# Attention with a threshold, then a feed-forward layer, on one core: scores from split q and k instead of float32 row halves

## The chip, the core and the metric

The kernel runs on one core of a Trainium2 chip. The core has five engines that each work through their own instructions in order: TensorE (PE, with its weight loads listed as PEld), VectorE (DVE), ScalarE (ACT), GpSimd (POOL) and SyncE (SP), which here issues all transfers. The metric is the device time of one execution in microseconds; the time before is the median of 3 runs, 1317.29 us (1316.47 to 1318.95).

## The reference

```
# q, k, v: (8, 8, 576, 64); w_in: (512, 2048); w_out: (2048, 512)
scores = scale * q @ k^T                       # scale = 64 ** -0.5
scores = where(scores >= max(scores) - tau, scores, -1e9)
attn   = exp(scores - max); attn /= sum(attn) + 1e-9
x      = (attn @ v), heads side by side        # 4608 x 512
out    = (s * relu(x @ w_in) ** 2 + b) @ w_out
```

## The kernel before

A **visit** is one batch entry, one pair of heads (2 of 8) and one half `u` of the first 512 query rows: 8 x 4 x 2 = 64 visits, four to a pair (batch, u). Each visit has four **tiles** of 128 query rows by 576 keys; half the visits have a fifth tile for the last 64 query rows of both heads (the tail). There are 288 tiles.

A tile goes through: scores on PE into a PSUM bank `s0` or `s1` (L205-222), scaling with the minimum on DVE into `sm` (L230), exp on ACT into `em` (L240), the threshold with the sum on DVE (L243), a reciprocal, the normalisation on POOL (L247), 32x32 block transposes on DVE into `tr` (L266, L268), and four transfers from `tr` to `er` which put the blocks in place (L272). The first four visits transpose on PE instead (L250-263). After a visit's last tile `with_v` multiplies v by `er` into `pv` (L284), and ACT copies the result to the x buffer `xb` (L288).

The scores are float32. k of both heads lies on the 128 partitions, 64 for each head, as does q; two products on the upper and lower rows of the array give a tile of each head (L220). The tail multiplies a block-diagonal `qd` by k (L211). `with_v` writes the two heads to the two column halves of the array.

The feed-forward layer (FFN) works on **blocks** of 256 rows: 16 full ones, one for each (batch, u), and two made of the tails (`xt`). A block is staged, that is, x is split into `xh` (rounded to float32r) and `xl` (the rest) by ACT and DVE (L398, L400). Then come 16 steps: 12 products of 256 columns into `h` (L415), relu, square and rounding on ACT (L418-421), the rest `gl` on POOL (L422), and 6 products of 512 columns into `o` (L428). There are three x buffers, and two pairs of `xh`/`xl`.

Nothing of the order is left to chance: all work is handed to `Plan` with an engine, a cost, keys that it reads and writes, and a due time `at` in tiles. `Plan.run` goes through it with these costs, gives each free engine the ready work with the smallest `at`, and so fixes each engine's order. SP's queue is ordered in the same way (L169).

Of the kernel before, what the change touches and what calls it, by code (L numbers as in the profile page):

```python
# [101 lines left out]
def tile_attention_ffn(ctx: ExitStack, tc: tile.TileContext, qT, kT, v, tau, w_in, w_out, s, b, out):  # L102
# [68 lines left out]

    class Visit:
        def __init__(self, n, bi, pair, u, tail):
            self.n, self.bi, self.pair, self.u, self.tail, self.end = n % 2, bi, pair, u, tail, False
# [4 lines left out]
            self.nb = (NB + (T if tail else 0)) // 32
            self.pe = n < PE_VISITS  # L180

        def load(self, at):
# [1 line left out]
            dma(295, lambda: nc.sync.dma_start(out=kb[n], in_=kT[bi, h2].rearrange("h d s -> (h d) s")), [], [("k", n)], at)
            dma(131, lambda: nc.sync.dma_start(out=qb[n], in_=qT[bi, h2, :, self.u * NB:(self.u + 1) * NB].rearrange(
                "h d s -> (h d) s")), [], [("q", n)], at)
            if self.tail:
                for j in range(2):
                    dma(16, lambda j=j: nc.sync.dma_start(out=qd[n][j * D:(j + 1) * D, j * T:(j + 1) * T],
                                                          in_=qT[bi, 2 * self.pair + j, :, M:S]), [], [self.kd[j]], at)  # L190
            for j in range(2):
                rows = "(p c) d -> p c d" if self.pe else "(c p) d -> p c d"
                dma(131, lambda j=j, rows=rows: nc.sync.dma_start(
                    out=vb[n][:, j, 0:NQ], in_=v[bi, 2 * self.pair + j, 0:M, :].rearrange(rows, p=P)),
                    [], [self.kv[j]], at + 1)
# [4 lines left out]
            for m in range(2):  # L200
                dma(16, lambda m=m: nc.sync.dma_start(  # L201
                    out=vb[n][:, :, NQ].rearrange("(k m) h d -> k m h d", m=4)[:, m],
                    in_=v[bi, h2, M + 32 * m:M + 32 * m + 32, :].rearrange("h k d -> k h d")), [], [self.kv[2 + m]], at + 1)
# [19 lines left out]

    def tile_of(vs, i, j, t):
        ps, ks_, st8 = bank[f"s{j}"], f"st{i % 6}", st[i % 6]
# [50 lines left out]
    def with_v(vs, at):  # L276
        n, nb = vs.n, vs.nb
        ps = bank["pv"]

        def products():  # L280
            for c in range(5):
                r = slice(0, T if vs.pe and c == NQ else P)
                for j in range(2):
                    nc.tensor.matmul(ps[j * D:(j + 1) * D, 0:32 * nb], vb[n][r, j, c], er[r, n, j, 0:nb, 32 * c:32 * c + 32],  # L284
                                     start=(c == 0), stop=(c == 4))
        pe(10.5 * 0.85 * 32 * nb, products, vs.kv + [("er", n, j, e) for j in range(2) for e in range(nb)], ["pv"], at)
        xk = xs[vs.bi, vs.u]
        act((340, 420), lambda: nc.scalar.copy(out=xb[xk][:, vs.pair], in_=ps[:, 0:NB]), ["pv"],  # L288
            [("x", xk, vs.pair)] + (["ident"] if xk == 2 else []), at)
# [26 lines left out]
    def weights(f, at):  # L316
# [6 lines left out]
        tag = ("xh", "xl")[f % 2] + ("01"[f // 2 % 2] if f < FIRST_WEIGHTS else "1")  # L323
# [19 lines left out]
        for u, k in (0, "i"), (1, "o"):  # L343
            kr, kt = (f"w{f}", k), (tag, u)
            act((665, 750), lambda u=u: nc.scalar.activation(
                out=tmp()[:, u], in_=words(1, u).bitcast(F32), func=AF.Prelu, scale=2.0 ** -112, alpha=-2.0 ** 32),
                [kr], [kt] if u else [tag, kt, (tag, 1)], at)
            dve2((480, 550), lambda u=u: nc.vector.tensor_scalar(
                out=y(u), in0=y(u), scalar1=3, scalar2=None, op0=ALU.logical_shift_left), [kt], [kt], at)
            dve2((700, 780), lambda u=u: nc.vector.scalar_tensor_tensor(  # L350
                out=y(u), in0=words(0, u), scalar=29, in1=y(u), op0=ALU.logical_shift_right, op1=ALU.bitwise_or),
                [kr, kt], [kt], at)
        for u, k in (0, "i"), (1, "o"):
            act((615, 700), lambda u=u: nc.scalar.copy(out=w()[:, u, 0], in_=tmp()[:, u]), [(tag, u)],
# [24 lines left out]

    class Block:  # L380
# [3 lines left out]
        def stage(self, at):  # L384

            k = count["stage"] % 2
            count["stage"] += 1
            self.kx = [f"xh{k}", f"xl{k}"]

            def get():  # L390
                if self not in lazy:
                    lazy[self] = [sb(t, [P, NC, NB], F32R) for t in self.kx]
                return lazy[self]
            self.get = get
            for c in range(0, NC, 2):
                sl = slice(c, c + 2)
                kh, kl = (self.kx[0], c // 2), (self.kx[1], c // 2)
                act((520, 620), lambda sl=sl: nc.scalar.copy(out=get()[0][:, sl], in_=self.src[:, sl]),  # L398
                    self.ksrc, [kh] if c else self.kx + [(x, u) for x in self.kx for u in range(2)], at)
                dve2((620, 700), lambda sl=sl: nc.vector.tensor_tensor(  # L400
                    out=get()[1][:, sl], in0=self.src[:, sl], in1=get()[0][:, sl].bitcast(F32), op=ALU.subtract),
                    self.ksrc + [kh], [kl], at)

        def step(self, f, at):
# [3 lines left out]
            kx = self.kx + [(x, c) for x in self.kx for c in range(2)]  # L408

            def products():  # L410
                xh, xl = self.get()
                i = 0
                for c in range(NC):
                    for w, x in ((wi[0][f], xh), (wi[0][f], xl), (wi[1][f], xh)):
                        nc.tensor.matmul(ps, w[:, c, :], x[:, c, :], start=(i == 0), stop=(i == 3 * NC - 1))  # L415
                        i += 1
            pe(3 * NC * 120.5, products, kx + [(f"w{f}", "i")], ["h"], at)
            act((290, 385), lambda: nc.scalar.activation(out=g, in_=ps, func=AF.Relu), ["h"], [f"g{k}"], at)  # L418
# [3 lines left out]
            do((715, 750), lambda: eng.tensor_tensor(out=lo, in0=g, in1=hi.bitcast(F32), op=ALU.subtract),  # L422
# [7 lines left out]
            for t in range(2):  # L430
                pe(3 * 232, lambda t=t: second(t), [f"gh{k}", f"gl{k}", (f"w{f}", "o")],
                   [("o", t)] + (["o"] if f == 0 and t == 0 else []), at + 1)

        def finish(self, at):
            for t in range(2):
                k, o = "oo", oo

                def take(t=t, o=o):
                    nc.vector.scalar_tensor_tensor(out=o, in0=bank["o"][:, t, :], scalar=s_t, in1=bias_t, op0=ALU.mult,  # L439
                                                   op1=ALU.add)  # L440
# [82 lines left out]
    for i, (vs, j, t) in enumerate(tiles):  # L523
        if t is None or not j:
# [76 lines left out]
```

## Time and profile before

| | |
|---|---|
| median of 3 runs | 1317.29 us |
| profiled execution | 1318.1 us, span 1316.1 us |
| mean granted clock of PE | 0.986 |
| DMA packets, bytes | 271470, 164.17 MB |
| issues of er, v, k, q, qd | 1088, 128 + 120 + 4, 64, 64, 64 |

The slices of the span show three parts:

```profile
PE   7689799999999999999999999999999999999997
DVE  6888876666676766657575656766666576663011
ACT  5666545545455555555455554555555455554343
PEclk8999899999999999999999999999999999999999
```

Each column is a fortieth of the span, 33 us, each digit a busy share in tenths. In the first five or six DVE is busiest, as the weights are converted beside the first visits. Then PE is. In the last three or four the attention is over (DVE falls to nothing), and the last FFN blocks run. A busy digit of PE doesn't say that it works at its peak: starts of products show that better. SP is not in these sums: what its queue does is read from its issues in order of time.

### The profile page before, as it was taken

How to read it: one execution, taken by the hardware profiler on the slowest of the kernel's cores; microseconds unless marked ns; L12 is line 12 of the kernel's file. 1: busy time of each engine (PE TensorE's matmuls, PEld its weight loads, DVE VectorE, ACT ScalarE, POOL GpSimd, SP SyncE). 2: the span in 40 equal slices, each digit the busy share in tenths (PEclk: the TensorE clock that was granted, in tenths of full speed). 3: DMA queues.
4: the chain of work that ended last, by engine and by line, in shares of the span. 5: the costliest groups of instructions: out<-in, count | busy, mean ns of one | idle time of the engine just before them, and what ended most of it. 6: DMA issues, size and time to landing. Idle time of an engine off the chain costs nothing.

```text
span 1316.1 us, 24095 instructions
## 1 busy us (share of the span) xinstructions
PE 1254.2 (95%) x7752; PEld 972.6 (74%) x7752; DVE 824.5 (63%) x2157; ACT 684.6 (52%) x1655; POOL 551.0 (42%) x613
## 2 busy tenths in 40 slices
PE   7689799999999999999999999999999999999997
PEld 5366567677677777777777777777787778787886
DVE  6888876666676766657575656766666576663011
ACT  5666545545455555555455554555555455554343
POOL 3676534344444444434344343534445344443210
PEclk8999899999999999999999999999999999999999
DMA  7844455545555455544454444544445444542000
GB/s 226 297 155 118 119 138 130 136 122 125 142 135 142 124 137 127 142 113 122 124 135 122 124 123 112 152 114 125 127 129 133 116 118 126 137 113 60 17 17 17
DMA packets 271470, 164.17 MB, mean 125 GB/s; under 512 B 99824, under 2 KB 256496, under 8 KB 271344
## 3 DMA queue, kind: packets, MB, share of 16 engines
q1 hardware_dynamic: 271344, 162.63, 46.5%
q8 instruction: 62, 1.02, 0.3%
q14 instruction: 64, 0.52, 0.1%
HBM read 63.96 MB, written 9.44 MB: 56 GB/s over the span
## 4 chain that ended last, share of the span: by engine, by line
PE 77%; DVE 7%; DMA 4%; SPq 4%; issue 3%; ACT 3%; POOL 1%; DVEq 0%; POOLq 0%; ACTq 0%
PE o L428 27%; PE h L415 27%; PE pv L284 12%; PE s L220 9%; SPq L272 3%; DMA er<-tr 3%; PE s L211 2%; DVE em L243 1%; DVE sm L230 1%; ACT em L240 1%; DMA out_dram<-oo 1%; DVE tr L266 1%; DVE xl L350 1%; DVE oo L439 1%; SPq L201 1%
## 5 line engine op out<-in xcount | busy, mean ns | idle before, releaser
L415 PE MATMUL h<-xh,w 128*128 128x256 f32 x2304 | 478.3, 290 | 18.7 <-ACT g L418 12.2
L247 POOL TENSOR_SCALAR em<-em,st,zero 128x576 f32<-128x576 f32 x288 | 283.2, 984 | 391.0 <-DVE st L246 236.7
L415 PEld LDWEIGHTS h<-xh,w 128*128 128x128 f32 x2304 | 379.4, 192 | 65.0 <-ACT g L420 20.4
L428 PE MATMUL o<-w,gh 128*128 128x512 f32 x1152 | 370.9, 403 | 3.4 <-DVE oo L439 3.4
L422 POOL TENSOR_TENSOR gl<-g,gh 128x256 fp32r<-128x256 f32 x272 | 222.7, 820 | 304.8 <-issue 136.1
L415 PE MATMUL h<-xl,w 128*128 128x256 f32 x1152 | 327.1, 284 | 0.3 <-DVE xl L400 0.3
L240 ACT ACTIVATE em<-sm,st 128x576 f32<-128x576 f32 x288 | 222.7, 774 | 192.7 <-DVE sm L230 125.7
L243 DVE SCALAR_TENSOR_TENSOR em<-sm,st,em 128x577 f32<-128x577 f32 x288 | 250.3, 870 | 89.0 <-ACT st L238 54.1
L230 DVE TENSOR_SCALAR_CACHE_REDUCE sm<-s,nsc 128x576 f32<-128x576 f32 x288 | 227.2, 808 | 121.6 <-PE s L220 83.4
L266 DVE STREAM_TRANSPOSE tr<-em 128x512 f32<-128x512 f32 x272 | 192.7, 709 | 144.9 <-DMA er<-tr 78.7
L428 PEld LDWEIGHTS o<-w,gh 128*128 128x128 f32 x1152 | 199.6, 189 | 68.1 <-issue 22.1
L418 ACT ACTIVATE g<-h 128x256 f32<-128x256 f32 x288 | 109.4, 380 | 266.2 <-PE h L415 258.9
L428 PE MATMUL o<-w,gl 128*128 128x512 f32 x576 | 225.5, 391 | 2.6 <-POOL gl L422 2.6
L415 PEld LDWEIGHTS h<-xl,w 128*128 128x128 f32 x1152 | 220.9, 192 | 8.4 <-DVE xl L400 0.6
L284 PE MATMUL pv<-er,v 128*64 128x256 f32 (+1 forms) x1280 | 185.2, 416 | 8.6 <-DMA er<-tr 5.4
L220 PE MATMUL s<-k,q 64*128 64x288 f32 x1024 | 167.0, 437 | 6.5 <-DVE sm L230 6.5
L284 PEld LDWEIGHTS pv<-er,v 128*64 128x64 f32 x1280 | 95.0, 138 | 87.1 <-issue 26.3
L428 PEld LDWEIGHTS o<-w,gl 128*128 128x128 f32 x576 | 108.2, 188 | 30.1 <-POOL gl L422 5.2
L220 PEld LDWEIGHTS s<-k,q 64*128 64x128 f32 x1024 | 93.3, 190 | 47.9 <-DVE sm L230 10.9
L421 ACT CAST gh<-g 128x256 fp32r<-128x256 f32 x288 | 115.8, 402 | 13.5 <-PE o L428 7.4
L420 ACT ACTIVATE g<-g 128x256 f32<-128x256 f32 x288 | 119.3, 414 | 6.5
L238 ACT ACTIVATE st<-st,tau 128x1 f32<-128x1 f32 x272 | 76.7, 286 | 26.3 <-DVE sm L230 26.0
(56 smaller groups left out, 532.2 us busy)
## 6 DMA issues: line engine op xcount, KB each, us to landing
er<-tr SPq DMA_DIRECT2D x1088, 80.0 KB, 2.2
k<-in_k_dram SPq DMA_DIRECT2D x64, 288.0 KB, 3.1
v<-in_v_dram SPq DMA_DIRECT2D x128, 128.0 KB, 2.5
q<-in_q_dram SPq DMA_DIRECT2D x64, 128.0 KB, 2.4
w<-in_moe_w_in_dram SPq DMA_DIRECT2D x16, 512.0 KB, 7.0
w<-in_moe_w_out_dram SPq DMA_DIRECT2D x16, 512.0 KB, 7.3
out_dram<-oo SPq DMA_DIRECT2D x32, 256.0 KB, 2.3
v<-in_v_dram SPq DMA_DIRECT2D x120, 16.0 KB, 2.1
```

The lines of the kernel that those rows point to most:

```text
L220: nc.tensor.matmul(bank[f"s{j}"][:, hf, 0:HS], qb[n][r, t * P:(t + 1) * P], kb[n][r, cs], start=True, stop=True)
L230: dve((745, 830), lambda: nc.vector.tensor_scalar(out=sb_[:, 0:S].rearrange("p (a b) -> p a b", a=2), in0=ps[:, :, 0:HS], scalar1=nsc, sca ...
L240: act((780, 870), lambda: nc.scalar.activation(out=ev, in_=sb_[:, 0:S], func=AF.Exp, bias=st8[:, 0:1], scale=-1.0), [sm_k, (ks_, 0)], [em_ ...
L243: dve2((940, 1010), lambda: nc.vector.scalar_tensor_tensor(out=eb, in0=sb_, scalar=st8[:, 1:2], in1=eb, op0=ALU.is_le, op1=ALU.mult, accum ...
L247: pool((900, 940), lambda: nc.gpsimd.tensor_scalar(out=ev, in0=ev, scalar1=st8[:, 4:5], scalar2=zero, op0=ALU.mult, op1=ALU.add), [em_k, ( ...
L266: nc.vector.transpose(out=to[:, :, 0:NQ].rearrange("p m c q -> p m (c q)"), in_=ev[:, 0:M].rearrange("p (m r) -> p m r", m=4))
L284: nc.tensor.matmul(ps[j * D:(j + 1) * D, 0:32 * nb], vb[n][r, j, c], er[r, n, j, 0:nb, 32 * c:32 * c + 32], start=(c == 0), stop=(c == 4))
L415: nc.tensor.matmul(ps, w[:, c, :], x[:, c, :], start=(i == 0), stop=(i == 3 * NC - 1))
L420: act((290, 390), lambda: nc.scalar.activation(out=g, in_=g, func=AF.Square), [f"g{k}"], [f"g{k}"], at)
L421: act((310, 405), lambda: nc.scalar.copy(out=hi, in_=g), [f"g{k}"], [f"gh{k}"], at)
L422: do((715, 750), lambda: eng.tensor_tensor(out=lo, in0=g, in1=hi.bitcast(F32), op=ALU.subtract), [f"g{k}", f"gh{k}"], [f"gl{k}"], at)
L428: nc.tensor.matmul(bank["o"][:, t, :], a[:, ts_], w, start=(f == 0 and i == 0), stop=(f == NF - 1 and i == 2))
```

## The change

From the ninth visit on (`FIRST_SPLIT = 8`, the second batch entry), scores are made in another way:

- Each head's k is loaded onto both partition halves, by two transfers, and so is its q, and its tail rows (`load_head`). ACT rounds k to float32r and POOL subtracts, which gives `khi` and `klo` on 128 partitions; of q the upper half keeps the rounded values, the lower half the rest (`prepare`, due 3.5 tiles ahead).
- A tile is then 4 products of 288 columns, (q rounded, q rest) on the whole array by `khi` and `klo` for two halves of the keys, into bank `s{i % 2}`; the tail is 8 products (`split_scores`). Tiles of one head stand together, where the heads alternated.
- Two x buffers instead of three, one pair of `xh`/`xl` instead of two; the first and last step of a block are cut into halves, so that staging can go half by half. The buffers of the split k take the place of the weights' scratch.
- Costs and due times in the plan change: second products are due 2.5 tiles after the first instead of 1.

```
+PE_VISITS, FIRST_SPLIT = 4, 8
+PREPARE_AHEAD = 3.5
...
-    xb = [const(f"x{i}", [P, NC, NB]) for i in range(3)]
+    qs = [const(f"qs{i}", [P, NB], F32R) for i in range(2)]
+    qt = const("qt", [P, 2, P], F32R)
+    xb = [const(f"x{i}", [P, NC, NB]) for i in range(2)]
...
+        def load_head(self, j, at):
+            bi, head = self.bi, 2 * self.pair + j
+            for o in 0, D:
+                dma(144, lambda o=o: nc.sync.dma_start(out=kb[j][o:o + D], in_=kT[bi, head]), [], [("rk", j, o)], at)
+            for o in 0, D:
+                dma(64, lambda o=o: nc.sync.dma_start(out=qb[j][o:o + D], in_=qT[bi, head, :, self.u * NB:(self.u + 1) * NB]),
+                    [], [("rq", j, o)], at)
+            if self.tail:
+                for o in 0, D:
+                    dma(16, lambda o=o: nc.sync.dma_start(out=qd[j][o:o + D, 0:T], in_=qT[bi, head, :, M:S]),
+                        [], [("rt", j, o)], at)
+
+        def prepare(self, j, at):
...
+            act((675, 760), lambda: nc.scalar.copy(out=part(0), in_=kb[j]), rk, [("khi", j)], at)
+            pool((1500, 1540), lambda: nc.gpsimd.tensor_tensor(out=part(1), in0=kb[j], in1=part(0).bitcast(F32),
+                                                               op=ALU.subtract), rk + [("khi", j)], [("klo", j)], at)
+            parts = [(qs[j], qb[j], rq, ("qs", j), (400, 480), (820, 850))]
...
+            for dst, src, kr, key, ca, cp_ in parts:
+                act(ca, lambda dst=dst, src=src: nc.scalar.copy(out=dst, in_=src), kr, [key], at)
+                pool(cp_, lambda dst=dst, src=src: nc.gpsimd.tensor_tensor(
+                    out=dst[D:P], in0=src[D:P], in1=dst[D:P].bitcast(F32), op=ALU.subtract), kr + [key], [key], at)
...
+    def split_scores(vs, i, j, t):
+        sk = f"s{i % 2}"
...
+        def products():
+            for hf in range(2):
+                cs = slice(hf * HS, (hf + 1) * HS)
+                for n, (stat, jj, k) in enumerate((stat, jj, k) for stat, jj in seq for k in range(2)):
+                    nc.tensor.matmul(bank[sk][:, hf, 0:HS], stat, lazy["k"][:, 2 * jj + k, cs],
+                                     start=(n == 0), stop=(n == 2 * len(seq) - 1))
...
-            k = count["stage"] % 2
+            first = not count["stage"]
...
+            if f in (0, NF - 1):
+                for c in range(0, NC, 2):
+                    pe(6 * 120.5, lambda c=c: products(range(c, c + 2)), [("xh", c // 2), ("xl", c // 2), (f"w{f}", "i")], ["h"], at)
...
-                   [("o", t)] + (["o"] if f == 0 and t == 0 else []), at + 1)
+                   [("o", t)] + (["o"] if f == 0 and t == 0 else []), at + 2.5)
```

What this does to the orders is seen on SP first. In the middle of the program SP's queue before held this, for about one visit (`tr_82` and `tr_83` are the two transposed tiles, `k_84` and `k_85`, `q_86` and `q_87`, `v_90` and `v_91` the two buffers of each input; the last column is the transfer's shape on its target side and how many stand in a row):

```order
L272 DMA er<-tr_82 128x1x160 x4
L272 DMA er<-tr_83 128x1x160 x4
L193 DMA v_90<-in_v_dram 128x4x64 x2
L201 DMA v_90<-in_v_dram 32x2x64 x2
L184 DMA k_85<-in_k_dram 128x576
L185 DMA q_87<-in_q_dram 128x256
L272 DMA er<-tr_82 128x1x160 x4
L272 DMA er<-tr_83 128x1x160 x4
```

And now, at a visit with a tail in the middle of the program (`qd_89` is one head's tail of q):

```order
L250 DMA v_91<-in_v_dram 32x2x64 x2
L337 DMA er<-tr_83 128x1x160 x4
L337 DMA er<-tr_82 128x1x160 x4
L203 DMA k_85<-in_k_dram 64x576 x2
L205 DMA q_87<-in_q_dram 64x256 x2
L209 DMA qd_89<-in_q_dram 64x64 x2
L337 DMA er<-tr_83 128x1x160 x4
L203 DMA k_84<-in_k_dram 64x576 x2
L205 DMA q_86<-in_q_dram 64x256 x2
L337 DMA er<-tr_82 128x1x160 x4
```

One load of k and one of q on 128 partitions for a visit have become two of k and two of q on 64 partitions for each head. In all SP has 1999 transfers where it had 1607.

POOL's queue before, where tiles of `em` alternate with FFN steps:

```order
L247 TENSOR_SCALAR em_81<-em_81,st_77,zero 128x576
L422 TENSOR_TENSOR gl_102<-g_98,gh_100 128x256
L247 TENSOR_SCALAR em_80<-em_80,st_72,zero 128x576
L422 TENSOR_TENSOR gl_103<-g_99,gh_101 128x256
L247 TENSOR_SCALAR em_81<-em_81,st_73,zero 128x576
```

And now (`k` is the split k, `qs` the split q, `qt` the split tail):

```order
L225 TENSOR_TENSOR qs_92<-q_86,qs_92 64x256
L312 TENSOR_SCALAR em_80<-em_80,st_76,zero 128x576
L218 TENSOR_TENSOR k<-k_84,k 128x576
L225 TENSOR_TENSOR qt<-qd_88,qt 64x64
L312 TENSOR_SCALAR em_81<-em_81,st_77,zero 128x576
L488 TENSOR_TENSOR gl_105<-g_101,gh_103 128x256
L488 TENSOR_TENSOR gl_106<-g_102,gh_104 128x256
L225 TENSOR_TENSOR qt<-qd_89,qt 64x64
```

The subtractions of the splits stand between two tiles' normalisations, so a tile waits behind them where their input is late.

More of the change, by code (lines that the diff above doesn't have):

```diff
@@ L170, in dma, with split_buffers, fn @@
         plan.add("SP", (max(550, kb_ * 3.6), 2200 + kb_ * 3.6), fn, r, w, at)
+    def split_buffers():
+        def fn():
+            lazy["k"] = sb("k", [P, 4, S], F32R)
+        old = [(t, "t", u) for t in ("k0", "k1") for u in range(2)] + ["ident"]
+        plan.add("-", (0, 0), fn, [], old + [(n, j) for n in ("khi", "klo") for j in range(2)], -100)
+        for n in range(2):
+            plan.add("-", (0, 0), lambda: None, [], [("k", n), ("q", n)] + [("qd", n, j) for j in range(2)] +
+                     [(x, n, o) for x in ("rk", "rq", "rt") for o in (0, D)], -100)
     class Visit:
@@ L222, in scores @@
         pe(1090, pairs, vs.kq, ["s0", "s1"], i - SCORES_AHEAD)
+    def split_scores(vs, i, j, t):
+        sk = f"s{i % 2}"
+        if t is None:
+            seq, keys = [(qt[:, jj], jj) for jj in range(2)], [("qt", 0), ("qt", 1)]
+        else:
+            seq, keys = [(qs[j][:, t * P:(t + 1) * P], j)], [("qs", j)]
+        def products():
[4 more added lines that the diff above has]
+                                     start=(n == 0), stop=(n == 2 * len(seq) - 1))
+        pe(535 * len(seq), products, keys + [(n, jj) for n in ("khi", "klo") for _, jj in seq], [sk], i - SCORES_AHEAD)
     def tile_of(vs, i, j, t):
-        ps, ks_, st8 = bank[f"s{j}"], f"st{i % 6}", st[i % 6]
+        sk = f"s{i % 2 if vs.split else j}"
+        ps, ks_, st8 = bank[sk], f"st{i % 6}", st[i % 6]
         sm_k, em_k, tr_k = f"sm{i % 2}", f"em{i % 2}", f"tr{i % 2}"
@@ L288, in with_v @@
         act((340, 420), lambda: nc.scalar.copy(out=xb[xk][:, vs.pair], in_=ps[:, 0:NB]), ["pv"],
-            [("x", xk, vs.pair)] + (["ident"] if xk == 2 else []), at)
+            [("x", xk, vs.pair)], at)
         if vs.tail:
@@ L316, in weights @@
     def weights(f, at):
-        tag = ("xh", "xl")[f % 2] + ("01"[f // 2 % 2] if f < FIRST_WEIGHTS else "1")
+        tag = ("xh", "xl", "k0", "k1")[f] if f < FIRST_WEIGHTS else ("k0", "k1")[f % 2]
         def words(k, u):
@@ L329, in tmp @@
             if ("tmp", f) not in lazy:
-                lazy["tmp", f] = sb(tag, [P, 2, DM], F32)
+                t = early[:, 2 * DM * int(tag[1]):2 * DM * (int(tag[1]) + 1)] if tag[0] == "k" else sb(tag, [P, 2 * DM], F32)
+                lazy["tmp", f] = t.rearrange("p (u n) -> p u n", u=2)
             return lazy["tmp", f]
@@ L343, in weights @@
         for u, k in (0, "i"), (1, "o"):
[L344 removed]
+            kr, kt = (f"w{f}", k), (tag, "t", u)
             act((665, 750), lambda u=u: nc.scalar.activation(
                 out=tmp()[:, u], in_=words(1, u).bitcast(F32), func=AF.Prelu, scale=2.0 ** -112, alpha=-2.0 ** 32),
[L347 removed]
+                [kr], [kt] if u else [kt, (tag, "t", 1)], at)
             dve2((480, 550), lambda u=u: nc.vector.tensor_scalar(
@@ L353, in weights @@
         for u, k in (0, "i"), (1, "o"):
-            act((615, 700), lambda u=u: nc.scalar.copy(out=w()[:, u, 0], in_=tmp()[:, u]), [(tag, u)],
+            act((615, 700), lambda u=u: nc.scalar.copy(out=w()[:, u, 0], in_=tmp()[:, u]), [(tag, "t", u)],
                 wkeys(f) if not u else [(f"w{f}", "o")], at)
@@ L378, in tile_attention_ffn, with xhl @@
     count = dict(stage=0, step=0)
+    def xhl():
+        if "xhl" not in lazy:
+            lazy["xhl"] = [sb(t, [P, NC, NB], F32R) for t in ("xh", "xl")]
+        return lazy["xhl"]
     class Block:
@@ L384, in stage @@
         def stage(self, at):
-            k = count["stage"] % 2
+            first = not count["stage"]
             count["stage"] += 1
[L388 to L394, printed above, removed]
+            more = [("xh", 1), ("xl", 0), ("xl", 1)] + [(x, "t", u) for x in ("xh", "xl") for u in range(2)] if first else []
             for c in range(0, NC, 2):
                 sl = slice(c, c + 2)
[L397 to L401, printed above, removed]
+                kh, kl = ("xh", c // 2), ("xl", c // 2)
+                act((617, 700), lambda sl=sl: nc.scalar.copy(out=xhl()[0][:, sl], in_=self.src[:, sl]),
+                    self.ksrc, [kh] + (more if not c else []), at)
+                dve2((850, 920), lambda sl=sl: nc.vector.tensor_tensor(
+                    out=xhl()[1][:, sl], in0=self.src[:, sl], in1=xhl()[0][:, sl].bitcast(F32), op=ALU.subtract),
                     self.ksrc + [kh], [kl], at)
@@ L407, in step, with products @@
             ps, g, hi, lo = bank["h"][:, 0:NB], gb[k], gh[k], gl[k]
[L408 to L418, printed above, removed]
+            def products(cs):
+                xh, xl = xhl()
+                for c in cs:
+                    for i, (w, x) in enumerate(((wi[0][f], xh), (wi[0][f], xl), (wi[1][f], xh))):
+                        nc.tensor.matmul(ps, w[:, c, :], x[:, c, :], start=(c == 0 and i == 0), stop=(c == NC - 1 and i == 2))
+            if f in (0, NF - 1):
+                for c in range(0, NC, 2):
+                    pe(6 * 120.5, lambda c=c: products(range(c, c + 2)), [("xh", c // 2), ("xl", c // 2), (f"w{f}", "i")], ["h"], at)
+            else:
+                pe(3 * NC * 120.5, lambda: products(range(NC)), [(x, c) for x in ("xh", "xl") for c in range(2)] + [(f"w{f}", "i")],
+                   ["h"], at)
+            act((378, 460), lambda: nc.scalar.activation(out=g, in_=ps, func=AF.Relu), ["h"], [f"g{k}"], at)
             eng, do = (nc.vector, dve2) if self.last else (nc.gpsimd, pool)
-            act((290, 390), lambda: nc.scalar.activation(out=g, in_=g, func=AF.Square), [f"g{k}"], [f"g{k}"], at)
-            act((310, 405), lambda: nc.scalar.copy(out=hi, in_=g), [f"g{k}"], [f"gh{k}"], at)
-            do((715, 750), lambda: eng.tensor_tensor(out=lo, in0=g, in1=hi.bitcast(F32), op=ALU.subtract),
+            act((400, 480), lambda: nc.scalar.activation(out=g, in_=g, func=AF.Square), [f"g{k}"], [f"g{k}"], at)
+            act((400, 480), lambda: nc.scalar.copy(out=hi, in_=g), [f"g{k}"], [f"gh{k}"], at)
+            do((800, 830), lambda: eng.tensor_tensor(out=lo, in0=g, in1=hi.bitcast(F32), op=ALU.subtract),
                [f"g{k}", f"gh{k}"], [f"gl{k}"], at)
@@ L467, in tile_attention_ffn @@
         vs.first = len(tiles)
-        tiles += [(vs, j, t) for t in range(2) for j in range(2)]
-        if vs.tail:
-            tiles.append((vs, 0, None))
+        if vs.split:
+            vs.heads = len(tiles), len(tiles) + 2
+            tiles += [(vs, 0, 0), (vs, 0, 1)] + ([(vs, 0, None)] if vs.tail else []) + [(vs, 1, 0), (vs, 1, 1)]
+        else:
+            tiles += [(vs, j, t) for t in range(2) for j in range(2)] + ([(vs, 0, None)] if vs.tail else [])
         vs.last = len(tiles) - 1
@@ L507, in tile_attention_ffn @@
         events.append((vs.first - 0.5 if n else -1, lambda vs=vs, n=n: n and vs.load(vs.first - LOAD_AHEAD)))
+        for j, i in enumerate(vs.heads if vs.split else ()):
+            events.append((i - 0.5, lambda vs=vs, j=j, i=i: (vs.load_head(j, i - LOAD_AHEAD), vs.prepare(j, i - PREPARE_AHEAD))))
+    events.append((visits[FIRST_SPLIT].first - 0.6, split_buffers))
     for n in range(2):
@@ L523, in tile_attention_ffn @@
     for i, (vs, j, t) in enumerate(tiles):
-        if t is None or not j:
+        if vs.split:
+            events.append((i, lambda vs=vs, i=i, j=j, t=t: split_scores(vs, i, j, t)))
+        elif t is None or not j:
             events.append((i, lambda vs=vs, i=i, t=t: scores(vs, i, t)))
```

42 lines of the change are left out of this document (27 added, 15 removed).

## The prediction

> **What bounds the kernel now.** I read the page's engine sums and slices first, then the table by stage, the waits of TensorE (PE), and last the queue of SyncE (SP), which the page's engine sums do not count.
>
> ```profile
> PE 1254.2 (95%) x7752; PEld 972.6 (74%) x7752; DVE 824.5 (63%) x2157; ACT 684.6 (52%) x1655; POOL 551.0 (42%) x613
> ...
> core 0: us, PE busy (x) PEld busy (x) DVE busy (x) ACT busy (x) POOL busy (x), PEclk, DMA share, GB/s
> 500.00:700.00 200.00, 198.56 (x1266) 154.77 (x1265) 129.05 (x347) 104.96 (x261) 84.75 (x96) 1.00 0.49 127
> 1100.00:1200.00 100.00, 100.00 (x648) 78.42 (x647) 62.44 (x170) 52.61 (x130) 42.27 (x48) 1.00 0.47 120
> ...
> PE pv L284 <- DMA er<-tr: 5.0, 5, 2.3
> PE o L428 <- DVE oo L439: 3.4, 5, 1.2
> PE h L415 <- ACT g L418: 3.3, 4, 1.7
> ```
>
> Columns of the table: the stretch, then each engine's busy time, clock and DMA share. From 500 us on PE is busy 99% of the stretch and waits almost for nothing (the last three rows cover 200 to 1200 us). DVE, ACT and POOL have room. So PE is the bound as the page sees it, and a lighter score product should shorten the run. But one more thing works in order: SP, which issues every transfer.
>
> ```profile
> L272 SPq DMA_DIRECT2D er<-tr x1088: 542/602/2056, 73.1 to 1203.3; - x182
> ...
> 626.16 0.54 SPq L185 DMA_DIRECT2D q<-in_q_dram  x1
> 626.80 5.07 SPq L272 DMA_DIRECT2D er<-tr  x8
> 631.97 1.14 SPq L193 DMA_DIRECT2D v<-in_v_dram  x2
> 633.20 1.33 SPq L201 DMA_DIRECT2D v<-in_v_dram  x2
> 634.62 2.51 SPq L272 DMA_DIRECT2D er<-tr  x4
> 637.24 0.54 SPq L184 DMA_DIRECT2D k<-in_k_dram  x1
> 637.82 1.15 SPq L189 DMA_DIRECT2D qd<-in_q_dram  x2
> 641.07 3.73 SPq L272 DMA_DIRECT2D er<-tr  x4
> ```
>
> Each row has start, duration, and how many issues are merged. From one start to the next: eight issues of er take 5.17 us, 0.646 each; two of v 1.23; two of its tail 1.42; one q 0.64; one k 0.58; two of qd about 1.24 with the gap behind. The first row says that one er issue takes 602 ns in the median and that they run from 73.1 to 1203.3 us. In that stretch the order of the program has behind the first er: 1088 er x 0.646 = 703 us, 116 v 71, 116 tails of v 82, 58 k 34, 58 q 37, 60 qd 37 and 36 stores of the output at about 0.63 (as q behind er) 23. **Sum 987 of 1130 us.** The queue is 87% full by its plain issue times. The 143 us left are waits and a few long issues (2056 ns is the longest, and four er took 3.73 us instead of 2.58):
>
> ```profile
> SPq L272 <- DVE st L246: 41.5, 49, 4.2
> ...
> SPq L272 <- DVE tr L268: 38.6, 19, 16.6
> SPq L193 <- PE pv L284: 23.1, 16, 6.4
> ```
>
> So there are two nearly full resources, PE and SP's queue. The change takes from one and gives to the other.
>
> **The change, part by part.** First PE.
>
> ```profile
> 617.86 0.28 PE L415 MATMUL h<-xh,w 128*128 128x256 f32 x1
> 618.07 1.24 PE L220 MATMUL s<-k,q 64*128 64x288 f32 x8
> 619.24 0.39 PE L415 MATMUL h<-xh,w 128*128 128x256 f32 x1
> 619.47 0.28 PE L415 MATMUL h<-xl,w 128*128 128x256 f32 x1
> 619.58 0.40 PE L415 MATMUL h<-xh,w 128*128 128x256 f32 x2
> 619.82 0.28 PE L415 MATMUL h<-xl,w 128*128 128x256 f32 x1
> ...
> 622.17 0.62 PE L428 MATMUL o<-w,gh 128*128 128x512 f32 x2
> 622.62 0.39 PE L428 MATMUL o<-w,gl 128*128 128x512 f32 x1
> ...
> 608.94 0.28 PE L415 MATMUL h<-xh,w 128*128 128x256 f32 x1
> 609.06 1.14 PE L211 MATMUL s<-k,qd 128*128 128x288 f32 x4
> 609.82 0.50 PE L415 MATMUL h<-xh,w 128*128 128x256 f32 x1
> 610.15 0.28 PE L415 MATMUL h<-xl,w 128*128 128x256 f32 x1
> ```
>
> Starts of float32r products of 256 columns lie 0.12 us apart (619.58 to 619.82 for two), those of 512 columns 0.225 (622.17 to 622.62). A line through both gives 0.133 for 288 columns, so a split tile of four costs 0.53 and two tiles 1.06. Before, a pair of tiles, with the change of kind on both sides, costs from 617.98 (617.86 + 0.12) to 619.35 (619.47 - 0.12), 1.37 us. Saved: 0.31 for each of 112 pairs, 35 us. A tail tile goes from 0.97 (609.06 to 610.15 - 0.12) to 8 x 0.133 = 1.06; 28 of them give back 2.5. **PE gains about 32 us**, if nothing else becomes late.
>
> Next ACT and POOL. For each of 112 heads the splits add a copy of 128x576 and one of 128x256 on ACT, and two subtractions on POOL; 56 small copies and subtractions come for the tails.
>
> ```profile
> L398 ACT CAST xh<-x 128x512 fp32r<-128x512 f32 x32 | 18.8, 624 | 0.0
> L288 ACT COPY x<-pv 128x256 f32<-128x256 f32 x64 | 23.8, 372 | 89.4 <-PE pv L284 89.2
> L356 POOL TENSOR_TENSOR w<-xh,w 128x512 fp32r<-128x512 f32 x16 | 23.3, 1472 | 3.3 <-ACT w L354 3.2
> L422 POOL TENSOR_TENSOR gl<-g,gh 128x256 fp32r<-128x256 f32 x272 | 222.7, 820 | 304.8 <-issue 136.1
> L400 DVE TENSOR_TENSOR xl<-x,xh 128x512 fp32r<-128x512 f32 x32 | 23.1, 750 | 3.9 <-ACT xh L398 3.8
> ```
>
> In proportion to the columns a head costs ACT 0.70 + 0.37 = 1.07 us and POOL 1.66 + 0.82 = 2.48. With some 0.2 and 0.3 for each tail copy: ACT 684.6 + 132 = 817, POOL 551.0 + 295 = 846. Both stay under two thirds of any time discussed here, so they bound nothing by themselves. What hides them is that a head is prepared at 3.5 tiles ahead and scored at one tile ahead, 2.5 tiles or some 10 us for a chain of about 3 us; a chain that loses this cover is a rival below. The single pair of split x: at each of 17 block changes a copy (0.62) and a subtraction (0.75) must come between the old block's last product and the new block's first, at least 1.4 and with the handovers some 1.6 us, at most 17 x 1.6 = 27 us. In the new order second products and a score tile stand in that place on PE, so I take nothing; without that cover, 27. Two x buffers instead of three delay one copy of pv until a block is staged; I take nothing, since FFN steps fill PE. The wider costs and the later due time of the second products change the order only; their effect is bounded by PE's 62 us of idle time below and by the 27 us above.
>
> Then **SP**. In visits 8 to 63 each head loads k twice and q twice, once for each half of the partitions, and its tail twice, where one load of k, one of q and two of qd served both heads. The order has 1999 transfers instead of 1607, 392 more. Behind the first er stand 2 k, 2 q and 448 half loads, 116 tail loads, and all the rest as before: 703 + 71 + 82 + 23 + 2 + 116 x 0.62 (72) = 953 us, and 448 times the price p of a half load. The trace has no load of k or q to 64 partitions. Nearest rows:
>
> ```profile
> 0.74 0.39 SPq L184 DMA_DIRECT2D k<-in_k_dram  x1
> 1.18 0.42 SPq L185 DMA_DIRECT2D q<-in_q_dram  x1
> ...
> 27.98 1.53 SPq L310 DMA_DIRECT2D w<-in_moe_w_in_dram  x3
> ...
> L189 SPq DMA_DIRECT2D qd<-in_q_dram x64: 480/594/1685, 42.9 to 1093.5; - x64
> ```
>
> At the start k to q is 0.44 from start to start. Three weight loads of 512 KB took 1.53, 0.51 each, so an issue does not get dearer with its bytes. qd, 16 KB on 64 partitions, takes 594 ns, no less than the 288 KB of k. So p lies between 0.44 and 0.65; qd is the only load on 64 partitions, so I take 0.60, nearer to it: 269 us, and the queue's sum becomes **1222 us instead of 987**.
>
> One rule speaks against these loads. The Trainium skill (DMA: Bandwidth & Descriptors, "Rules for kernel authors") says that splitting a transfer into two partition halves is not worth it, since both halves share the same 16 DMA engines. By that alone the sum would hardly move: the trace has the DMA engines at half load (0.49 above), and 23 MB more on 164 leave them there. The price here is the issue.
>
> The 143 us of waits and long issues: long issues go with the number of issues, while many waits on DVE go, since a late queue finds its tiles ready. Between 60 and 180 (143 x 1222/987 = 177), I take 112. **Sum:** 73 until the first er, 1222 + 112, and from the last er to the end 113 as before (1316.1 - 1203.3; the order has 32 FFN steps behind the last pv, as against 33): 1520 us. PE, with 1254 - 32 = 1222 us of work, then has idle time, and its 32 us are hidden. The profiled run took 1318.1 us around its span of 1316.1, the median is 1317.29, so 1520 + 2 - 1 = 1521; I say 1520.
>
> **Rivals.**
> 1. *The issue time bends and PE stays the bound.* An issue may be long only because the one before it is still in hand. If the average slot fell from 0.63 to under 0.54 us (1924 issues x 0.54 = 1039; with 60 of rest that is just the 1286 - 73 - 113 = 1100 us that PE would need between first and last er), PE would decide: 1318 - 32 = **1286**, faster. For it: the first k and q at 0.44. Against it: 1088 er at 602 ns in the median, at a DMA share of one half. 5%. The Trainium skill (DMA: Bandwidth & Descriptors, "Issuing engines are not separate DMA queues") calls the issue time usually small beside the transfer; by that rule this rival would be the outcome. The trace has 0.60 us issues in a queue that has hardly a gap.
> 2. *The gain is given back by the single pair of split x*, on top of rival 1: 1286 + 27 = **1313**, with the price of some waits no change. 3%.
> 3. *The split chain adds its own wait.* Where k comes late, POOL stands in its subtraction, and the next tile's em, behind it in POOL's queue, comes late too, so SP's next er. At 1.0 us for each of 112 heads: 1520 + 112 = **1632**. For it: POOL works in order, and SP is late. Against it: the loads stand several tiles ahead. 9%.
> 4. *Half loads are cheap* (p of 0.44) and most waits go (60): 1520 - 72 - 52 = **1396**. 6%.
>
> **How the numbers follow.** Forecast, SP's queue as the bound, 77%: 1520. Its ends are 1520 - 72 - 52 = 1396 and 1520 + 22 + 68 = 1610 (p 0.65, rest 180). The range is 1400 to 1620: nearly all of the forecast, some half of rivals 3 and 4, so 8 in 10. Rivals 1 and 2 lie below it, the other half of 3 above. A measurement of this kernel tells 0.2% (2.6 us) from no change. Faster 5%, same 3%, slower 92%.
>
> **What would show it.** After: SP issues without gaps from 100 us to the last er, which stands at about 1400; half loads of 0.5 to 0.6 us; PE busy near 80%, waiting at pv for the landing of er; DVE waiting for er to free tr. Four split products in 0.53 us between float32r neighbours would confirm PE's term. I am wrong if the last er stands near 1200, if half loads take under 0.4, or if PE stays at 95%.

## The result, and the profile after

| | before | after |
|---|---|---|
| median of 4 runs | 1318.12 us (1316.47 to 1319.47) | 1513.88 us (1508.59 to 1514.31) |
| ratio | | 1.1477 (95% interval 1.1447 to 1.1506) |
| profiled span, clock of PE | 1316.1 us, 0.986 | 1512.4 us, 0.944 |

The change makes the kernel 15% slower. The page of the changed kernel gives the engines' sums and the chain that ended last:

```profile
PE 1307.9 (86%) x7864; PEld 1063.5 (70%) x7864; DVE 844.0 (56%) x2157; ACT 784.2 (52%) x1935; POOL 810.7 (54%) x894
...
PE 39%; SPq 18%; DMA 15%; DVE 10%; issue 9%; POOL 5%; ACT 4%; DVEq 0%; POOLq 0%; ACTq 0%
SPq L337 14%; DMA er<-tr 12%; PE o L494 12%; PE h L477 11%; PE pv L349 11%; PE s L284 3%; DVE em L308 3%; DVE sm L295 2%; DVE tr L331 2%; SPq L250 2%; POOL em L312 2%; SPq L205 1%; POOL gl L488 1%; ACT em L305 1%; POOL k L218 1%
```

The same line of the page of before:

```profile
PE 77%; DVE 7%; DMA 4%; SPq 4%; issue 3%; ACT 3%; POOL 1%; DVEq 0%; POOLq 0%; ACTq 0%
```

PE's share of the chain has halved. SP's queue (SPq) and the transfers (DMA) together went from 8% to 33%, and no engine is as full as PE was. Where PE stands still is read from its waits between 200 and 1390 us (who waited, for whom; us in total, times, longest):

```profile
PE pv L349 <- DMA er<-tr: 87.7, 39, 5.1
PE h L477 <- ACT g L484: 35.7, 23, 4.9
```

What holds DVE is read from the waits over the whole span, and, for the kernel before, from the end of the page's row of its transposes:

```profile
DVE tr L331 <- DMA er<-tr: 209.2, 117, 5.4
```

```profile
L266 DVE STREAM_TRANSPOSE tr<-em 128x512 f32<-128x512 f32 x272 | 192.7, 709 | 144.9 <-DMA er<-tr 78.7
```

PE waits 87.7 us for er at pv, where it waited 5.0 us before (200 to 1200 us); DVE waits 209 us for the er transfers to free `tr` (78.7 us before). Both pages give 2.2 us from the issue of an er to its landing, so what is late is the issue. SP's issues, by their lines (min/median/max ns, first and last start in us):

```profile
L337 SPq DMA_DIRECT2D er<-tr x1088: 542/596/2024, 73.6 to 1403.2; - x182
...
L203 SPq DMA_DIRECT2D k<-in_k_dram x224: 465/586/1480, 138.8 to 1363.1; - x112
...
L205 SPq DMA_DIRECT2D q<-in_q_dram x224: 465/542/1872, 140.1 to 1367.1; - x112
...
L209 SPq DMA_DIRECT2D qd<-in_q_dram x112: 518/547/1282, 144.0 to 1281.9; - x112
```

and SP's timeline in the middle of the run:

```profile
717.88 1.19 SPq L203 DMA_DIRECT2D k<-in_k_dram  x2
719.16 2.46 SPq L209 DMA_DIRECT2D qd<-in_q_dram  x4
721.71 0.54 SPq L509 DMA_DIRECT2D out_dram<-oo  x1
722.34 1.10 SPq L203 DMA_DIRECT2D k<-in_k_dram  x2
723.53 1.23 SPq L337 DMA_DIRECT2D er<-tr  x2
```

There is no gap here: each row starts within 0.1 us of the end of the one before. Two half loads of k take 1.28 us from start to start, four tail loads 2.55, that is 0.64 each.

PE's own term can be read as well, from PE's timeline of the changed kernel:

```profile
642.90 0.28 PE L477 MATMUL h<-xh,w 128*128 128x256 f32 x1
643.02 1.23 PE L284 MATMUL s<-k,qs 128*128 128x288 f32 x8
644.09 0.28 PE L477 MATMUL h<-xh,w 128*128 128x256 f32 x1
...
651.10 1.22 PE L284 MATMUL s<-k,qt 128*128 128x288 f32 x8
652.15 0.28 PE L477 MATMUL h<-xh,w 128*128 128x256 f32 x1
```

Two split tiles take 1.07 us, with nothing lost on either side, and a tail tile 1.05. PE's work is lighter by about what was forecast; the time is lost elsewhere.

### The profile page after: what moved, and what is told of

Read it like the earlier page. It is cut to its first block, busy times and chain, and to the rows that moved or that the text cites. A ratio compares the mean times of both kernels' runs of the same rounds, so it can differ in the third digit from the quotient of the medians.

```text
span 1512.4 us, 26555 instructions
## 1 busy us (share of the span) xinstructions
PE 1307.9 (86%) x7864; PEld 1063.5 (70%) x7864; DVE 844.0 (56%) x2157; ACT 784.2 (52%) x1935; POOL 810.7 (54%) x894
## 3 DMA queue, kind: packets, MB, share of 16 engines
q1 hardware_dynamic: 295536, 187.43, 46.8%
## 4 chain that ended last, share of the span: by engine, by line
PE 39%; SPq 18%; DMA 15%; DVE 10%; issue 9%; POOL 5%; ACT 4%; DVEq 0%; POOLq 0%; ACTq 0%
SPq L337 14%; DMA er<-tr 12%; PE o L494 12%; PE h L477 11%; PE pv L349 11%; PE s L284 3%; DVE em L308 3%; DVE sm L295 2%; DVE tr L331 2%; SPq L250 2%; POOL em L312 2%; SPq L205 1%; POOL gl L488 1%; ACT em L305 1%; POOL k L218 1%
## 5 line engine op out<-in xcount | busy, mean ns | idle before, releaser
L477 PEld LDWEIGHTS h<-xh,w 128*128 128x128 f32 x2304 | 386.9, 194 | 67.9 <-ACT g L484 51.5
L312 POOL TENSOR_SCALAR em<-em,st,zero 128x576 f32<-128x576 f32 x288 | 272.0, 945 | 269.3 <-DVE st L311 217.2
L477 PE MATMUL h<-xl,w 128*128 128x256 f32 x1152 | 330.7, 287 | 8.9 <-DVE xl L464 8.9
L308 DVE SCALAR_TENSOR_TENSOR em<-sm,st,em 128x577 f32<-128x577 f32 x288 | 272.2, 946 | 98.2 <-ACT st L303 50.2
L349 PE MATMUL pv<-er,v 128*64 128x256 f32 (+1 forms) x1280 | 241.1, 475 | 98.8 <-DMA er<-tr 89.6
L295 DVE TENSOR_SCALAR_CACHE_REDUCE sm<-s,nsc 128x576 f32<-128x576 f32 x288 | 230.6, 804 | 113.1 <-PE s L284 112.4
L349 PEld LDWEIGHTS pv<-er,v 128*64 128x64 f32 x1280 | 119.4, 157 | 199.5 <-issue 127.3
L218 POOL TENSOR_TENSOR k<-k,k 128x576 fp32r<-128x576 f32 x112 | 164.7, 1471 | 57.6 <-ACT k L217 51.6
L284 PE MATMUL s<-k,qs 128*128 128x288 f32 x896 | 156.3, 301 | 8.6 <-DVE sm L295 8.5
L284 PEld LDWEIGHTS s<-k,qs 128*128 128x128 f32 x896 | 140.5, 192 | 28.8 <-DVE sm L295 10.6
```

What stands on the lines that cost most here:

```text
L218: pool((1500, 1540), lambda: nc.gpsimd.tensor_tensor(out=part(1), in0=kb[j], in1=part(0).bitcast(F32), op=ALU.subtract), rk + [("khi", j)] ...
L284: nc.tensor.matmul(bank[sk][:, hf, 0:HS], stat, lazy["k"][:, 2 * jj + k, cs], start=(n == 0), stop=(n == 2 * len(seq) - 1))
L295: dve((745, 830), lambda: nc.vector.tensor_scalar(out=sb_[:, 0:S].rearrange("p (a b) -> p a b", a=2), in0=ps[:, :, 0:HS], scalar1=nsc, sca ...
L308: dve2((940, 1010), lambda: nc.vector.scalar_tensor_tensor(out=eb, in0=sb_, scalar=st8[:, 1:2], in1=eb, op0=ALU.is_le, op1=ALU.mult, accum ...
L312: pool((900, 940), lambda: nc.gpsimd.tensor_scalar(out=ev, in0=ev, scalar1=st8[:, 4:5], scalar2=zero, op0=ALU.mult, op1=ALU.add), [em_k, ( ...
L477: nc.tensor.matmul(ps, w[:, c, :], x[:, c, :], start=(c == 0 and i == 0), stop=(c == NC - 1 and i == 2))
```

## The experiments

**1. More issues, nothing else.** The kernel before, with the loads of k and q issued in quarters.

```
-dma(295, lambda: nc.sync.dma_start(out=kb[n], in_=kT[bi, h2].rearrange("h d s -> (h d) s")), ...)
+def quarters(dst, src):
+    for o in range(0, P, 32):
+        nc.sync.dma_start(out=dst[o:o + 32], in_=src[o // D, o % D:o % D + 32])
+dma(295, lambda: quarters(kb[n], kT[bi, h2]), [], [("k", n)], at)     # q likewise
```

> The kernel before, where each visit's load of k and of q is issued as four loads of 32 partitions (same bytes; PE, ACT, POOL and DVE do the same work as before). Theory, SP's issue queue is the bound: behind the first er 58 x (8 x 0.64 - 1.22) = 226 us more issue time, 987 + 226 = 1213, with some 90 us of rest 73 + 1213 + 90 + 113 = 1489 us; if a load of 32 partitions costs as little as one of 128 partitions behind another (0.48), 1415. Rival, what costs in the change is its split chain on ACT and POOL or the buffers: nothing of that is here, so 1318. Rival, transfers cost by their bytes: 1318.

Measured: 1443.36 us, ratio 1.0967 (1.0936 to 1.0998). Same bytes, same work on the four other engines, and 126 us more, so the additional issues cost it. The size lies between the two that were expected; SP's timeline of this run shows the prices.

```profile
605.23 1.73 SPq L186 DMA_DIRECT2D k<-in_k_dram  x4
607.06 2.49 SPq L274 DMA_DIRECT2D er<-tr  x4
609.59 1.99 SPq L186 DMA_DIRECT2D q<-in_q_dram  x4
611.68 2.49 SPq L274 DMA_DIRECT2D er<-tr  x4
...
L274 SPq DMA_DIRECT2D er<-tr x1088: 542/602/1891, 82.8 to 1326.9; - x182
```

Four quarters of k take 1.83 us here, four of q 2.09. Over the whole trace the median from start to start is 0.58 us for a quarter behind an er and 0.47 for one behind another quarter, 1.99 for four. So k and q cost 2 x 1.99 where they cost 1.22: 58 x 2.76 = 160 us, and the queue's sum is 987 + 160 = 1147. From 82.8 to 1326.9 are 1244 us; 97 are left as waits and long issues, where the expectation had 90.

**2. The change without its split scores.**

```
-PE_VISITS, FIRST_SPLIT = 4, 8
+PE_VISITS, FIRST_SPLIT = 4, 64
```

> The changed kernel with FIRST_SPLIT = 64, so that no visit uses split scores; two x buffers, one pair of split x, the halved first and last steps and the later second products stay. Theory, the half loads on SP cost the time: 1318, at most 1345 if the single pair of split x takes its 27 us, some 1312 if the later second products save PE's waits in the last stretch. Rival, the buffers hold the attention back: most of the 196 us stay, over 1450.

Measured: 1318.11 us, ratio 1.0008 (0.9993 to 1.0024). Two x buffers, one pair of split x, the halved steps and the later second products cost nothing that can be measured, nor do they gain. The loss belongs to the split scores and their loads.

**3. and 4. One transfer with a doubled source.**

```
-for o in 0, D:
-    dma(144, lambda o=o: nc.sync.dma_start(out=kb[j][o:o + D], in_=kT[bi, head]), ...)
+def twice(src):
+    return src.unsqueeze(0).broadcast_to([2] + list(src.shape))
+dma(288, lambda: nc.sync.dma_start(out=kb[j], in_=twice(kT[bi, head])), ...)   # q, tails likewise; 4: nc.scalar
```

> The changed kernel, where each head's k, q and tail rows reach both partition halves by one transfer of 128 partitions with a doubled source instead of two of 64; still on SP, same bytes, all splits and products as in the change. Theory, SP's queue: 224 loads at 0.48 to 0.64 instead of 448 at 0.64, 56 tails fewer; 953 - 35 + 108 to 143 = 1026 to 1061, and with 90 us of rest 73 + 1061 + 90 + 113 = 1337 us (1302 with the cheap price). Rival, the split chain on ACT and POOL costs the time: it is unchanged, so 1500. Rival, the DMA engines' bytes: 1514.

> As the one before, with these loads (112 of k, 112 of q, 56 tails) issued by ACT instead of SP. Theory: SP's issues fall to 953 - 72 = 881 us, less than before, so PE is the bound again with its saving of 32 us: 1286 to 1300, unless ACT (784 us busy and 280 issues of about 0.6 us, 952) makes the tiles late. Rival, the split chain costs: over 1450.

Measured: 1913.36 us (ratio 1.4535) and 1928.67 us (1.4672). Both theories missed, and so did the rivals. The chain of run 3 and SP's timeline in it show where the time goes:

```profile
DMA 38%; PE 28%; SPq 12%; DVE 8%; issue 6%; POOL 4%; ACT 2%; DVEq 0%; POOLq 0%; ACTq 0%
...
719.71 0.54 SPq L204 DMA_DIRECT2D k<-in_k_dram  x1
720.37 0.54 SPq L205 DMA_DIRECT2D q<-in_q_dram  x1
721.02 7.46 SPq L334 DMA_DIRECT2D er<-tr  x6
```

The loads issue in 0.54 us, but six er issues behind them take 7.46 us instead of 3.9. The trace also records each packet that the DMA engines move. In the 97 of these loads of k whose packets stand alone there, 2.1 packets are in hand at a time, and a load's 128 packets take 6.3 us (medians); in the changed kernel 84 pairs of halves move their 128 packets in 1.6 us, 10.6 at a time. The Trainium skill (DMA: Bandwidth & Descriptors, "Why a DMA increments its semaphore by 16 and not by 1") says that the number of DMA engines is the largest, up to 16, that divides the slowest dimension of both sides; a doubled source has a slowest dimension of 2. The 2.1 packets agree. In run 4 an er issue has its 602 ns again (median), but SP stands still 363 us before er issues, in waits that the profile puts down to the landing of k and q; why er should wait for these isn't shown. So these two runs answer another question than the one asked, and the next two load in another form:

**5. and 6. One plain transfer of 128 rows.** q and k lie in DRAM a second time, each head's 64 rows twice, so that one load fills both halves.

```
+dma(288, lambda: nc.sync.dma_start(out=kb[j], in_=k2[bi, head]), ...)                            # 5
+plan.add("ACT", (600, 3236), lambda: nc.scalar.dma_start(out=kb[j], in_=k2[bi, head]), ...)      # 6
```

> The changed kernel, where q and k lie in DRAM a second time with each head's rows twice one behind the other, so that one plain transfer of 128 rows fills both partition halves; 112 loads of k, 112 of q and 56 tails on SP instead of 448 and 112. All splits and products as in the change. Theory, SP's issue queue: 917 for the rest + 224 x 0.46 to 0.64 = 1020 to 1060, and with 90 us of rest 73 + 1040 + 90 + 113 = 1316 us (1297 to 1336). Rival, the split chain on ACT and POOL costs the time: 1500, unchanged. Rival, one load for both halves is slow in itself, as in the run with the doubled source (1913).

> As the one before, with these 280 loads issued by ACT. Theory: SP's issues fall to 881 us, PE is the bound with 32 us less work than before: 1286 to 1300. Rival, what is left of the change (split chain, one x pair, ACT's 280 issues of 0.55 us) binds: 1320 or more.

Measured: 1346.44 us, ratio 1.0216 (1.0186 to 1.0246), and 1319.67 us, 1.0030 (1.0006 to 1.0054). With all splits left in place, 167 us of the loss go when 280 of the 560 issues go, and 194 when the other 280 leave SP too. The split chain on ACT and POOL is the same in all three kernels, so these 167 and 194 us are not its cost. In run 5 the queue reads:

```profile
L202 SPq DMA_DIRECT2D k<-in_k_dram x112: 327/536/1881, 138.5 to 1190.3; - x112
...
L335 SPq DMA_DIRECT2D er<-tr x1088: 542/596/2289, 72.3 to 1233.5; - x182
```

A k behind an er takes 0.63 and a q behind a k 0.49, so 917 + 112 x 1.12 = 1042 of 1161 us; 119 are rest, not 90. That is the 30 us by which the expectation missed: waits came back, as gaps of over 0.13 us between SP's issues add up to 87 us, where the changed kernel has 43. In run 6 the theory was wrong by more: SP has room and PE less work, and still nothing is gained.

```profile
PE pv L347 <- DMA er<-tr: 9.8, 11, 2.0
PE o L492 <- DVE oo L503: 6.9, 6, 3.9
PE pv L347 <- DMA q<-in_q_dram: 5.4, 3, 2.0
...
500.00:800.00 300.00, 289.15 (x1880) 246.18 (x1879) 198.47 (x505) 180.73 (x459) 197.09 (x217) 0.99 0.56 146
```

PE is busy 289 of 300 us (96%), as against 198.56 of 200 before (99%), and the first and third row name pv as the main place, 15 us where it was 5.0. They do not see all of it: added up from each pv product's start to the next product's, pv holds PE 214 us in run 6 and 189 us in the kernel before.

**7. The same half loads, on ACT.**

```
-dma(144, lambda o=o: nc.sync.dma_start(out=kb[j][o:o + D], in_=kT[bi, head]), [], [("rk", j, o)], at)
+plan.add("ACT", (600, 2720), lambda o=o: nc.scalar.dma_start(out=kb[j][o:o + D], in_=kT[bi, head]), ...)
```

> The changed kernel with its own 560 half loads (64 partitions, two for each thing), all issued by ACT instead of SP; the transfers are the same. Theory, the place in SP's order costs the time and not the transfers: SP falls to 881 us; ACT rises to 784 + 560 x 0.55 = 1092 us, still under PE's work, so 1290, or up to 1400 if ACT's issues make tiles late. Rival, the halves cost something that both queues share (the DMA engines, or the unit that makes their descriptors): 1480 to 1514.

Measured: 1404.91 us, ratio 1.0660 (1.0606 to 1.0714). The transfers are those of the change; 109 of its 196 us go with their place. What is left shows in ACT's order, in waits of this run:

```profile
L203 ACTq DMA_DIRECT2D k<-in_k_dram x224: 472/500/2202, 130.8 to 1252.0; - x112
...
POOL k L218 <- ACT k L217: 184.7, 77, 9.7
DVE em L308 <- ACT st L303: 142.1, 89, 8.0
```

In the changed kernel these two waits were 51.6 and 50.2 us. A half load costs ACT 500 ns (median); a tile's small operation on ACT, behind some of them, comes late. Whether the two queues also hinder each other isn't told apart by this run.

**8. to 11. The true price of an issue in the plan.** The plan believed an er issue to take 450 ns, and fixed PE's order by that. The two numbers of a cost are the engine's own time and the time until the result is there.

```
# 8, 10 and 11: er, then SP's other loads and stores
-plan.add("SP", (450, 2600), ...)
+plan.add("SP", (646, 2850), ...)
-plan.add("SP", (max(550, kb_ * 3.6), 2200 + kb_ * 3.6), fn, r, w, at)
+plan.add("SP", (640, 2300 + kb_ * 3.6), fn, r, w, at)
# 8 and 10: the loads that ACT issues; k, and q and tails likewise
-plan.add("ACT", (600, 3236), ...)
+plan.add("ACT", (380, 3236), ...)
# 9 and 10; in these FFN_AFTER is 3.5 instead of 2.5
-SCORES_AHEAD, VALUES_AFTER = 1, 2
+SCORES_AHEAD, VALUES_AFTER = 1, 3
```

> The run with loads of 128 rows on ACT (1319.7 us), with the plan's costs for SP set to what the traces show: 646 ns for an er issue instead of 450, 640 for other loads instead of 550 or more, 380 for an issue on ACT. Theory: with SP relieved, PE's saving of 32 us was eaten by its waits, most at pv for er (loss at pv 34 us between 200 and 1190, 14 before), since the plan believes er earlier than it is; with the right costs pv is placed later and 10 to 25 us come back: 1295 to 1310. Rival, the tile chain through DVE, ACT and POOL is at its limit: 1320.

> The same run of 1319.7 us with the values due three tiles behind a visit instead of two (and the FFN one tile later). Theory: PE no longer waits at pv, some 20 us of its 34 come back: 1300. Rival, a wait at pv only moves into the v loads and the x buffers behind it: 1320 or more.

> Both edits together. Theory: 1290 to 1305, not more than PE's 1286 allows. Rival: as the better of the two alone.

> The kernel before with the same true costs of SP in its plan. PE is the bound there and waits 28 us in all between 200 and 1190, so at most 10 us come: 1308 to 1318.

| run | median us | ratio to before |
|---|---|---|
| 8: run 6 with true costs | 1281.82 | 0.9734 (0.9717 to 0.9751) |
| 9: run 6, values a tile later | 1305.93 | 0.9908 (0.9886 to 0.9930) |
| 10: both | 1280.86 | 0.9732 (0.9718 to 0.9746) |
| 11: the kernel before with true costs | 1293.51 | 0.9822 (0.9809 to 0.9836) |

Run 9 came near its theory (1300). Runs 8 and 10 beat theirs, and run 11 gained 23 us where at most 10 were expected. Its windows show where; the first fence has the kernel before, the second run 11, the third run 10, for the same two stretches:

```profile
200.00:500.00 300.00, 290.29 (x1788) 220.13 (x1788) 200.13 (x541) 151.90 (x374) 123.53 (x139) 0.99 0.51 133
500.00:800.00 300.00, 296.88 (x1882) 232.14 (x1881) 191.95 (x521) 158.66 (x392) 126.87 (x144) 1.00 0.48 125
```

```profile
200.00:500.00 300.00, 296.86 (x1882) 229.43 (x1882) 208.66 (x568) 161.79 (x396) 120.92 (x147) 1.00 0.53 138
500.00:800.00 300.00, 299.46 (x1912) 234.06 (x1910) 196.90 (x528) 157.63 (x394) 127.15 (x144) 1.00 0.50 128
```

```profile
200.00:500.00 300.00, 293.15 (x1935) 247.93 (x1934) 220.12 (x575) 194.98 (x487) 218.43 (x236) 1.00 0.63 166
500.00:800.00 300.00, 293.21 (x1939) 248.55 (x1938) 205.42 (x525) 187.61 (x475) 205.49 (x224) 1.00 0.58 151
```

In run 11 PE does 1882 products from 200 to 500 us where it did 1788, and 1912 from 500 to 800 us, where it did 1882 and is now busy 299.46 of 300 us; the last er stands at 1178.6 instead of 1203.3. Two SP costs were changed there, each in both of its numbers, and no run tells which of them gains. In run 8 pv holds PE 186 us again (214 in run 6), as its theory said. Run 10 is the fastest of all: 1280.86, below both kernels. It holds the split scores, but against run 11, which has the old scores, it gains 13 us of the 32 that PE saves. Some 10 of the other 19 us are idle time of PE, 13.6 us in these two stretches where run 11 has 3.7; the rest stays open.

**12. The change itself with true costs.** The edit to SP's costs of run 8, half loads on SP.

> The changed kernel itself, half loads on SP, with the true costs of SP in its plan. Theory, the issues themselves fill the queue and no order can hide them: behind the first er 953 + 448 x 0.64 = 1240 us of issue time and some 40 us of long issues remain, so at least 73 + 1240 + 40 + 113 = 1466; 1470 to 1505. Rival, the loss is a planning error, the plan believing SP faster than it is, and the issues can be hidden: 1320 to 1400.

Measured: 1501.88 us, ratio 1.1421 (1.1378 to 1.1465).

```profile
L337 SPq DMA_DIRECT2D er<-tr x1088: 542/602/1946, 69.9 to 1388.6; - x182
```

1240 of these 1319 us are issue time, 79 are rest. A plan that knows the price gains 12 us against the change and no more: the issues themselves fill the queue.

## Why the prediction was right

- *Two nearly full resources.* Right. SP's queue, outside the page's engine sums, became the bound; run 1 shows it by adding issues, runs 5 to 7 by leaving SP fewer or none of them, and run 12 shows that the wrong costs in the plan were not the cause.
- *PE gains 32 us.* The size is right (1.07 and 1.05 us, forecast 1.06), and it was hidden as said. The 1.37 us of a pair before came from one pair; over the 126 pairs of the trace the median is 1.36. Runs 8 and 11, 12 us apart, show that the saving is worth part of that once SP has room.
- *ACT and POOL.* The new groups are busy 132 us on ACT, as forecast, and 276 on POOL (forecast 295); 12.7 and 19.0 of this are the tails, the rest these rows:

```profile
L217 ACT CAST k<-k 128x576 fp32r<-128x576 f32 x112 | 75.0, 669 | 30.8 <-DMA k<-in_k_dram 22.7 <-PE s L284 6.9 <-DMA er<-tr 0.9
L224 ACT CAST qs<-q 128x256 fp32r<-128x256 f32 x112 | 44.8, 400 | 31.1 <-DMA q<-in_q_dram 25.5 <-PE s L284 2.9 <-PE o L494 2.2
...
L218 POOL TENSOR_TENSOR k<-k,k 128x576 fp32r<-128x576 f32 x112 | 164.7, 1471 | 57.6 <-ACT k L217 51.6 <-PE s L284 2.5 <-PE o L494 0.7
L225 POOL TENSOR_TENSOR qs<-q,qs 64x256 fp32r<-64x256 f32 x112 | 92.4, 825 | 21.8 <-ACT qs L224 10.7 <-issue 2.0 <-POOL em L312 0.6
```

  The chain does wait for late loads (22.7 and 25.5 us on ACT), rival 3 in small; run 5 keeps the chain and is rid of most of the loss, so it did not decide.
- *One pair of split x, two x buffers: nothing.* Right, by run 2.
- *SP's sum.* The total came out right by two misses that cancel. The price of a half load was 0.64, not 0.60 (18 us more: 1240 us of issues); waits and long issues left 1403.2 - 73.6 - 1240 = 90 us, not 112. The reason given for 112 holds by half. Waits did go: gaps of over 0.13 us between issues add up to 43 us between first and last er, where the kernel before has 112. Long issues did not grow with the number of issues: 51 before and 54 now take over 0.9 us, 43 and 42 us beyond 0.6 each. The sum also counts 36 stores where 32 stand before the last er in both traces, which is 2.5 us. The last er was forecast at 73 + 1222 + 112 = 1407 and stands at 1403.2; from there to the end are 109 us, not 113.
- *What would show it.* PE waiting at pv, DVE waiting for `tr`: as forecast. SP's issues are nearly without gaps, but for these 43 us. PE busy near 80% was not right: the page has 86%, 1307.9 us where the forecast had 1222 of work. It rose from 1254.2 by 54 us, and pv's products, which wait for er, alone rose by 56. The products of `h` from `xh` kept their mean length (289 ns, before 290), though the mean granted clock is lower (0.944, before 0.986). So a busy sum can hold waiting. The first row is of the kernel before:

```profile
L284 PE MATMUL pv<-er,v 128*64 128x256 f32 (+1 forms) x1280 | 185.2, 416 | 8.6 <-DMA er<-tr 5.4
```

```profile
L349 PE MATMUL pv<-er,v 128*64 128x256 f32 (+1 forms) x1280 | 241.1, 475 | 98.8 <-DMA er<-tr 89.6
```

- *Rival 1.* An issue did not get shorter in a fuller queue: er has 596 ns in the median, 602 before. What the Trainium skill says in DMA: Bandwidth & Descriptors, "Issuing engines are not separate DMA queues", that an issue is usually small beside its transfer, does not carry here: 0.60 us of issue stand beside 2.2 us to landing, and it was the issues that filled the queue. Its advice against partition halves does (same page, "Rules for kernel authors"), though the DMA engines were no busier (46.5% before, 46.8% after) and the price was the issue.

## What to carry to other kernels

Count the transfers that one queue issues and multiply by the slot from start to start; a queue that is in no engine's sum can be the fullest resource. A transfer's price in such a queue does not follow its bytes, so cutting each transfer into two about doubles what the queue pays. And a plan that orders work by costs should have measured ones: setting SP's costs to them gained 1.8% on a kernel whose PE looked 99% busy from 500 us on.

## What the runs showed that I had not expected

- Half loads of k and q, 64 partitions each, cost 0.64 us from start to start. Their quarters of 32 partitions in run 1 cost 0.47 behind one another, and a load of q on 128 partitions behind one of k costs 0.49 in run 5. The partitions alone do not set it: in the changed kernel v's loads of 128 partitions (shape 128x4x64) cost 0.60 behind one another, and v's tails of 32 partitions 0.70. Why stays open.
- SP's long issues come with packets of 16 KB on queue 8, which the page lists as of kind `instruction`. Of the 51 issues of over 0.9 us between the first and the last er of the kernel before, 50 have such a packet at their start (its own start lies 0.10 us earlier in the median), and 53 of the 54 in the changed kernel (0.16 us). No run changes these packets, so that they hold the issue up is not shown.
- A source with a repeated outer dimension of two moves with two packets in hand instead of ten, and in run 3 slows the er issues behind it: 1913 us instead of 1346 in run 5.
- A correction of costs in the plan alone was worth 23 us in run 11 (two costs of SP) and 38 us in run 8 against run 6 (these two and that of an issue on ACT), which is more than PE's whole saving of 32 us in the change.
